# Five neighbouring weight rows to a partition in a fused layernorm, attention and gated-MLP kernel

## The chip, the cores and the metric

The kernel runs on one core of a Trainium2 chip. A core has a matrix engine (TensorE, PE in the profile; its weight loads are shown apart as PEld), a vector engine (VectorE, DVE), an activation engine (ScalarE, ACT), a general engine (GpSimd, POOL) and a queue processor that issues most transfers (SyncE, SP). The metric is the device time of one execution in microseconds. Before the change it is 308.31 us, the median of three runs (308.24 to 308.45).

## What is computed

The input x has 2048 rows (positions) of 640 features in bf16. The layernorm of x, called xn, feeds two branches, and the output is their sum with x:

```python
x = A_x
xn = _layernorm(x, axis=-1)
return x + _A_ref(xn, A_wqkv, A_wo) + _B_ref(xn, B_w_gate, B_w_up, B_w_down)
# A: qkv = xn @ wqkv (640 x 1920); 32 heads of 20; causal attention over a window
#    of 256 positions; the heads' outputs @ wo (640 x 640)
# B: (sigmoid(xn @ w_gate) * (xn @ w_up)) @ w_down, with 1536 hidden columns
```

The products with wqkv, w_gate and w_up sum over the 640 features. They are the ones that the change touches: such a sum can take the features in any order, as long as xn and the weight use the same one.

## The kernel before

**Tiling.** The 2048 positions are four chunks (c = 0 to 3) of 512, each of four blocks (s) of 128. The 640 features are cut into five tiles of 128 (DC = 5, index d), since a matmul sums over at most the 128 partitions. Tile d holds the features 128 d to 128 d + 127: feature f lies at partition f mod 128 of tile f div 128. All weights are loaded once and stay on chip as `[128 partitions, 5 tiles, columns]`. `wqkv_r` (line 163) is the view of the QKV weight that its loads take: `load_v` (line 181) reads the columns of V in two halves of 320, `load_wqkv` (line 171) those of Q and of K, 640 each, and `load_gu` (line 201) reads the gate and up weights, 384 columns at a time. In each of these loads a partition gets five pieces, one from each of five rows of the weight; a piece is 640, 1280 or 768 bytes long, which is only a part of its row (3840 bytes in wqkv, 3072 in gate and up).

**How xn gets its features onto partitions.** For chunk 0, at the start of the kernel, `transpose_rows` (line 296) has TensorE transpose each block: five transposes, each with 128 columns of the normed rows as the stationary operand (a PEld weight load) and an identity streaming through, then one copy out of PSUM into `xnT`. For the chunks 1 to 3, `g_norms` (line 385) takes the statistics of four blocks on VectorE and then norms them in `norm_block` (line 286), which writes the features of a row in the order "quarter q, tile b, 32 places f". `store_rows` puts these rows into a DRAM scratch, and `load_quarters` (line 305) reads them back, one quarter to 32 partitions. VectorE's 32 x 32 transposes in `turn_block` (line 313) then leave partition 32 q + f of tile b with the feature wanted. Between the last norm of a chunk and its `xnT` lie a store, a load and four turns.

**Order of the work.** The schedule is written by hand: the program order on every engine is the order in which the functions are called. At the start the queue SP issues the loads of x blocks 0, 1 and 3, the first half of V's weight, x block 2, the second half, Q and K, and then the first parts of gate and up. TensorE meanwhile runs some dummy matmuls (`keep_warm`), the transposes of block 0 and block 1, the first V product `v00` (line 695, ten steps of the loop at line 368 with block 1's), block 3's transposes, further V products, and so on; then the Q and K products of chunk 0 (`proj_block`, line 324). After that a generator machine (`Fill`) interleaves the attention steps with the pieces of everything else: gate/up of chunk 0, the norms and turns of chunk 1 beside them (lines 735 to 737), Q/K and V of chunk 1, the output of chunk 0, and so on. PSUM results lie in four buffers of `ps_d`, freed by copies on VectorE and ScalarE.

For chunk 0 the Q and K weights are read with a stride: `proj_block` views a slot of `wqk` as `"p (k m) -> p m k"`, so that consecutive columns of the stationary operand lie five elements (10 bytes) apart. For the later chunks GpSimd has sorted the columns (`sort_columns`) and they lie next to each other.

Of the kernel before, what the change touches and what calls it, by code (L numbers as in the profile page):

```python
# [9 lines left out]
P = 128  # L10
# [5 lines left out]
DC = D // P  # L16
# [10 lines left out]
FS = 768  # L27
# [85 lines left out]
def kernel(  # L113
# [11 lines left out]
    nc = tc.nc  # L125
# [34 lines left out]

    wqk = const.tile([P, 2 * DC + 1, D], BF16, name="wqk")
    wv = const.tile([P, DC, D], BF16, name="wv")
    wqkv_r = A_wqkv.rearrange("(c p) n -> p c n", p=P)
    wg = [const.tile([P, DC, FS], BF16, name=f"wg{k}") for k in range(F // FS)]
    wu = [const.tile([P, DC, FS], BF16, name=f"wu{k}") for k in range(F // FS)]
    wd = const.tile([P, FC, D], BF16, name="wd")
# [33 lines left out]

    def load_gu(t, w, k, lo=0, hi=FS):
        nc.sync.dma_start(out=t[k][:, :, lo:hi],
                          in_=w.rearrange("(c p) f -> p c f", p=P)[:, :, k * FS + lo:k * FS + hi])

    load_gu(wg, B_w_gate, 0, 0, FS // 2)
    load_gu(wu, B_w_up, 0, 0, FS // 2)
    clear("q")
    clear("k")
    load_gu(wg, B_w_gate, 0, FS // 2)

    def load_rest():
# [23 lines left out]
    ident = const.tile([P, P], BF16, name="ident")  # L235
# [27 lines left out]
    xns = {}  # L263
# [22 lines left out]
    def norm_block(c, s, mv, rstd):  # L286
        xn = lnp.tile([P, D], BF16, name="xn")
        made, of = xn, xc[c][:, s, :]
        if c:
            made = xn.rearrange("p (q b f) -> p b q f", q=4, b=DC)  # L290
            of = of.rearrange("p (b q f) -> p b q f", q=4, b=DC)
        nc.vector.tensor_scalar(out=made, in0=of, scalar1=mv[:, 0:1],
                                scalar2=rstd[:, 0:1], op0=SUB, op1=MULT)
        xns[c, s] = xn

    def transpose_rows(s, copy, lo=0, hi=DC):
        pt = ps_h.tile([P, DC, P], BF16, name="pt")
        for d in range(lo, hi):
            nc.tensor.transpose(pt[:, d, :], xns[0, s][:, d * P:(d + 1) * P], ident)  # L299
        copy(out=xnT[0][:, lo:hi, s * P:(s + 1) * P], in_=pt[:, lo:hi, :])  # L300

    def store_rows(c, s):
# [82 lines left out]
    def g_norms(c, behind=0):  # L385


        mvs = lnp.tile([P, SBC, nc.vector.BN_AGGR_DIM], FP32, name="mvs", bufs=1)
        for s in range(SBC):
            ln_block(c, s, mvs[:, s, :])  # L390
            if s < SBC - 1:
                yield 0
        for _ in range(behind):
            yield 0
        rstds = rstd_blocks(mvs)
        for _ in range(4):
            yield 0
        for s in range(SBC):
            norm_block(c, s, mvs[:, s, :], rstds[:, s:s + 1])
            store_rows(c, s)  # L400
            if s < SBC - 1:
                yield 0
# [126 lines left out]
    def scores(c, step):  # L529
        pt = pp.tile([P, HG, PTW], BF16, name="pT")  # L530
        ps = ps_s.tile([P, HG, CW], FP32, name="ps")
        for o, j, q, n, col in sorted(step["pieces"], key=lambda x: -x[3]):
            kc, kb = divmod(c * CW // U + j, CW // U)
            for a in range(2):
                for i in range(HG):
                    nc.tensor.matmul(  # L536
                        ps[a * U:(a + 1) * U, i, col * U:(col + n) * U],
                        lhsT=qk["k", kc, o // GH][32 * i:32 * i + DH, o % GH + a, kb * U:(kb + 1) * U],
                        rhs=qk["q", c, o // GH][32 * i:32 * i + DH, o % GH + a, q * U:(q + n) * U],
                        start=True, stop=True)  # L540
        nc.scalar.activation(out=pt[:, :, 0:CW], in_=ps, func=EXP, scale=SCALE)  # L541
        for diag, u, n in step["masks"]:
            base, sign = (0, 1) if diag else (-1, -1)
            for a in range(2):
                two = pt[a * U:(a + 1) * U].rearrange("p h (a b) -> p h a b", a=2)
                k, b = divmod(u, SPAN)
                view = two[:, :, k:k + n, b * U:(b + 1) * U]
                nc.gpsimd.affine_select(out=view, in_=view, pattern=[[0, HG], [0, n], [sign, U]],  # L548
                                        compare_op=GE, fill=0.0, base=base, channel_multiplier=-sign)
        if "late" not in step:  # L550
            return pt, None
        view = pt[:, :, step["late"] * U:(step["late"] + 2) * U]
        return pt, lambda: nc.vector.tensor_tensor(out=view, in0=view, in1=edge, op=MIN)
# [103 lines left out]
    def norm(s, mv, r):  # L657
        nc.vector.reciprocal(r, r)
        norm_block(0, s, mv, r)
# [29 lines left out]
    for lo, hi in ((0, 3), (3, DC)):  # L689
        transpose_rows(0, act, lo, hi)  # L690
    keep_warm(7)
    norm_act(1, xn1, neg1, r1)
    mv3 = ln_mv(ln_half(0, 3, 1, stats3))
    transpose_rows(1, dve)
    v00 = project_v(0, 0, 0)
    r3 = root(mv3)
# [3 lines left out]
    v10 = project_v(0, 1, 0)  # L700
    copy_v(0, 0, 0, v00, dve, (0,))
    transpose_rows(3, dve)
    v01 = project_v(0, 0, 1)
    norm_act(2, xn2, neg2, r2)
# [59 lines left out]
    for t, (c, k, step) in enumerate(todo):  # L764
# [11 lines left out]
        pt, late = scores(c, step)  # L776
# [13 lines left out]
    c = NCH - 1  # L790
# [62 lines left out]
```

## Time and profile before

| | us |
|---|---|
| median of three runs | 308.31 (308.24 to 308.45) |
| the profiled execution: its time | 308.43 |
| the profiled execution: its span on the core | 306.7 |
| VectorE busy in the span | 179.9 (59%) |
| ScalarE busy | 197.5 (64%) |
| GpSimd busy | 173.0 (56%) |
| DMA, all queues: bytes moved, mean rate | 36.04 MB, 118 GB/s |

The profile is of one execution. A busy time is the time in which an engine runs instructions. The chain of waits is found by going back from the last instruction, at each step to what released it. A row of the groups gives a line of the kernel, the engine, the operation, the tiles (written <- read), the shapes and the count; then the busy time in us and the mean of one in ns; then the idle time of the engine just before them and what ended it. A row of a timeline begins with the start and the length, in us from the span's start.

### The profile page before, as it was taken

How to read it: one execution, taken by the hardware profiler on the slowest of the kernel's cores; microseconds unless marked ns; L12 is line 12 of the kernel's file. 1: busy time of each engine (PE TensorE's matmuls, PEld its weight loads, DVE VectorE, ACT ScalarE, POOL GpSimd, SP SyncE). 2: the span in 40 equal slices, each digit the busy share in tenths (PEclk: the TensorE clock that was granted, in tenths of full speed). 3: DMA queues.
4: the chain of work that ended last, by engine and by line, in shares of the span. 5: the costliest groups of instructions: out<-in, count | busy, mean ns of one | idle time of the engine just before them, and what ended most of it. 6: DMA issues, size and time to landing. Idle time of an engine off the chain costs nothing.

```text
span 306.7 us, 10106 instructions
## 1 busy us (share of the span) xinstructions
PE 299.9 (98%) x4341; PEld 168.0 (55%) x4376; DVE 179.9 (59%) x356; ACT 197.5 (64%) x194; POOL 173.0 (56%) x314
## 2 busy tenths in 40 slices
PE   8999999999999999999999999999999999999996
PEld 6654444445657654554557654554546664444774
DVE  5735657889866569683826555482733527362433
ACT  6833768688965648888655538979585557778000
POOL 3086667479873728676572827657372756557000
DMA  7998959646574152773001222650000210000202
GB/s 209 364 316 253 320 185 260 206 129 194 141 231 111 44 161 83 235 221 75 4 0 47 65 70 80 193 177 2 2 2 2 66 45 25 0 4 0 88 24 64
DMA packets 40148, 36.04 MB, mean 118 GB/s; under 512 B 9000, under 2 KB 39848, under 8 KB 40104
## 3 DMA queue, kind: packets, MB, share of 16 engines
q1 hardware_dynamic: 39240, 34.63, 37.1%
q10 hardware_dynamic: 864, 0.77, 0.8%
q8 instruction: 34, 0.56, 0.8%
q14 instruction: 10, 0.08, 0.1%
HBM read 24.77 MB, written 10.62 MB: 115 GB/s over the span
## 4 chain that ended last, share of the span: by engine, by line
PE 96%; DMA 2%; issue 1%; SPq 0%; DVE 0%
PE y L481 18%; PE pu L467 17%; PE pg L460 17%; PE pqk L331 14%; PE ps L536 9%; PE pv L368 8%; PE y L488 7%; PE acc L567 6%; DMA wv<-in_A_wqkv_dram 2%; SPq L177 0%; PE pt L299 0%; DVE xn L492 0%
## 5 line engine op out<-in xcount | busy, mean ns | idle before, releaser
L548 POOL TENSOR_SCALAR_AFFINE_SELECT pT<-pT 64x512 bf16<-64x512 bf16 (+1 forms) x252 | 152.4, 605 | 90.7 <-ACT pT L541 79.0
L541 ACT ACTIVATE pT<-ps 128x2048 bf16<-128x2048 f32 x75 | 140.8, 1877 | 58.8 <-PE ps L536 57.8
L471 DVE SCALAR_TENSOR_TENSOR h<-th,pu 128x512 bf16<-128x512 f32 x48 | 32.7, 683 | 55.9 <-PE pu L467 42.7
L467 PE MATMUL pu<-xnT,wu 128*128 128x512 bf16 x230 | 58.9, 380 | 0.7 <-issue 0.3
L460 PE MATMUL pg<-xnT,wg 128*128 128x512 bf16 x225 | 58.3, 380 | 1.2 <-issue 0.6
L481 PE MATMUL y<-wd,h 128*128 128x320 bf16 (+2 forms) x396 | 56.6, 295 | 0.0
L331 PE MATMUL pqk<-xnT,wqk 128*128 128x512 bf16 x190 | 44.9, 380 | 0.7 <-issue 0.3
L481 PEld LDWEIGHTS <-h 128*128 128x128 bf16 x396 | 36.7, 98 | 15.9 <-issue 2.2
L463 ACT ACTIVATE th<-pg 128x512 f32<-128x512 f32 x48 | 28.6, 596 | 15.3 <-PE pg L460 15.1
L460 PEld LDWEIGHTS <-wg 128*128 128x128 bf16 x240 | 22.2, 98 | 25.7 <-issue 2.0
L467 PEld LDWEIGHTS <-wu 128*128 128x128 bf16 x240 | 22.1, 98 | 25.4 <-issue 1.8
L536 PE MATMUL ps<-qT,kT 20*64 20x320 bf16 (+4 forms) x1456 | 31.9, 259 | 0.0
L331 PEld LDWEIGHTS <-wqk 128*128 128x128 bf16 x200 | 19.5, 103 | 21.2 <-issue 1.2
L579 DVE STREAM_TRANSPOSE t<-acc 128x512 f32<-128x512 f32 x32 | 21.1, 695 | 13.7 <-PE acc L567 13.7
L536 PEld LDWEIGHTS <-kT 20*64 20x64 bf16 x1456 | 15.7, 103 | 24.5 <-issue 22.0
L492 DVE SCALAR_TENSOR_TENSOR rows<-y,rows 128x320 bf16<-128x320 f32 x30 | 14.3, 484 | 21.4 <-PE y L488 21.1
L368 PE MATMUL pv<-wv,xnT 128*128 128x320 bf16 x160 | 25.8, 300 | 0.3 <-DMA wv<-in_A_wqkv_dram 0.3
L488 PE MATMUL y<-wo,oc 128*128 128x320 bf16 (+2 forms) x165 | 24.2, 295 | 0.0
L567 PE MATMUL acc<-pT,v 64*32 64x320 bf16 (+4 forms) x1456 | 19.7, 252 | 0.0
L567 PEld LDWEIGHTS <-v 64*32 64x32 bf16 x1456 | 16.4, 91 | 5.9 <-ACT pT L541 1.3
L368 PEld LDWEIGHTS <-xnT 128*128 128x128 bf16 x160 | 14.6, 98 | 8.9 <-issue 1.6
L591 DVE TENSOR_TENSOR on<-t,rec 128x320 bf16<-128x320 f32 (+1 forms) x32 | 18.6, 580 | 1.1
(52 smaller groups left out, 187.8 us busy)
## 6 DMA issues: line engine op xcount, KB each, us to landing
qT<-sq SPq DMA_DIRECT2D x16, 256.0 KB
kT<-sk SPq DMA_DIRECT2D x16, 256.0 KB
sq<-st SPq DMA_DIRECT2D x20, 128.0 KB
sk<-st SPq DMA_DIRECT2D x20, 128.0 KB
out_dram<-rows SPq DMA_DIRECT2D x15, 160.0 KB
wg<-in_B_w_gate_dram SPq DMA_DIRECT2D x4, 480.0 KB
wu<-in_B_w_up_dram SPq DMA_DIRECT2D x4, 480.0 KB
xc<-in_A_x_dram SPq DMA_DIRECT2D x3, 640.0 KB
```

The lines of the kernel that those rows point to most:

```text
L331: nc.tensor.matmul(ps, lhsT=wt[:, m, :], rhs=xnT[c][:, d, :], start=(d == 0), stop=(d == DC - 1))
L368: nc.tensor.matmul(ps[:, 0:HALF], lhsT=xnT[c][:, d, s * P:(s + 1) * P], rhs=wv[:, d, hf * HALF:(hf + 1) * HALF], start=(d == 0), stop=(d = ...
L460: nc.tensor.matmul(pg, lhsT=part(wg, d, f), rhs=xnT[c][:, d, :], start=(d == 0), stop=(d == DC - 1))
L463: nc.scalar.activation(out=th, in_=pg, func=TANH, scale=0.5)
L467: nc.tensor.matmul(pu, lhsT=part(wu, d, f), rhs=xnT[c][:, d, :], start=(d == 0), stop=(d == DC - 1))
L471: nc.vector.scalar_tensor_tensor(out=h, in0=th, scalar=1.0, in1=pu, op0=ADD, op1=MULT)
L481: nc.tensor.matmul(y[:, 0:cut[1] - cut[0]], lhsT=ht[c, f][:, s * P:(s + 1) * P], rhs=wd[:, f, cut[0]:cut[1]], start=(f == 0), stop=False)
L488: nc.tensor.matmul(y[:, 0:cut[1] - cut[0]], lhsT=oc[c, m][:, s * P:(s + 1) * P], rhs=wo[:, m, cut[0]:cut[1]], start=False, stop=(m == DC - 1))
L536: nc.tensor.matmul(ps[a * U:(a + 1) * U, i, col * U:(col + n) * U], lhsT=qk["k", kc, o // GH][32 * i:32 * i + DH, o % GH + a, kb * U:(kb + ...
L541: nc.scalar.activation(out=pt[:, :, 0:CW], in_=ps, func=EXP, scale=SCALE)
L548: nc.gpsimd.affine_select(out=view, in_=view, pattern=[[0, HG], [0, n], [sign, U]], compare_op=GE, fill=0.0, base=base, channel_multiplier ...
L567: nc.tensor.matmul(acc[32 * i:32 * i + 32, q * U:(q + n) * U], lhsT=vt[kb][a * U:(a + 1) * U, u, h * VW:h * VW + 32], rhs=pt[a * U:(a + 1) ...
```

## The change

The rows of wqkv, w_gate and w_up go to partitions five neighbours at a time: partition p now gets the rows 5 p to 5 p + 4, in the tiles 0 to 4, where it had the rows p, 128 + p, 256 + p, 384 + p and 512 + p. Feature f thus lies at partition f div 5 of tile f mod 5. The columns that each load takes, the order of the loads and the number and size of the pieces are as before.

xn follows. In `norm_block`, for the chunks 1 to 3, the row of x is read in the order "quarter, 32 places, tile" and written where it was written before, so that consecutive elements written are five elements apart in what is read. In `transpose_rows`, for chunk 0, the 128 columns of a transpose are taken five elements apart. `turn_block`, `load_quarters`, all matmuls and the weights wd and wo are as they were.

```diff
-    wqkv_r = A_wqkv.rearrange("(c p) n -> p c n", p=P)
+    wqkv_r = A_wqkv.rearrange("(p c) n -> p c n", p=P)
...
         nc.sync.dma_start(out=t[k][:, :, lo:hi],
-                          in_=w.rearrange("(c p) f -> p c f", p=P)[:, :, k * FS + lo:k * FS + hi])
+                          in_=w.rearrange("(p c) f -> p c f", p=P)[:, :, k * FS + lo:k * FS + hi])
...
         made, of = xn, xc[c][:, s, :]
         if c:
             made = xn.rearrange("p (q b f) -> p b q f", q=4, b=DC)
-            of = of.rearrange("p (b q f) -> p b q f", q=4, b=DC)
+            of = of.rearrange("p (q f b) -> p b q f", q=4, b=DC)
         nc.vector.tensor_scalar(out=made, in0=of, scalar1=mv[:, 0:1],
                                 scalar2=rstd[:, 0:1], op0=SUB, op1=MULT)
...
         pt = ps_h.tile([P, DC, P], BF16, name="pt")
+        by_row = xns[0, s].rearrange("p (k d) -> p d k", d=DC)
         for d in range(lo, hi):
-            nc.tensor.transpose(pt[:, d, :], xns[0, s][:, d * P:(d + 1) * P], ident)
+            nc.tensor.transpose(pt[:, d, :], by_row[:, d, :], ident)
         copy(out=xnT[0][:, lo:hi, s * P:(s + 1) * P], in_=pt[:, lo:hi, :])
```

## The prediction

> **What bounds the kernel now.** I read the page's busy times and its chain first, then the waits, then the timeline of the first 14 us, where the changed loads and transposes run, and last the groups of the norms and turns.
>
> ```profile
> PE 299.9 (98%) x4341; PEld 168.0 (55%) x4376; DVE 179.9 (59%) x356; ACT 197.5 (64%) x194; POOL 173.0 (56%) x314
> ...
> PE 96%; DMA 2%; issue 1%; SPq 0%; DVE 0%
> ```
>
> TensorE runs for 299.9 of 306.7 us, and the chain that ended last is 96% TensorE. The change takes no matmul away. It can gain only from the 6.8 us in which TensorE stands, and the one DMA in the chain is one that it touches: the first half of V's weight.
>
> ```profile
> 5.30 0.45 PE L299 MATMUL pt<-ident,xn 128*128 128x128 bf16 x5
> 5.59 0.57 PE L247 MATMUL pwarm<-const-bfloat16-1.0 128*128 128x128 bf16 x7
> 6.44 0.45 PE L299 MATMUL pt<-ident,xn 128*128 128x128 bf16 x5 [0.28 <-DVE xn L675]
> 7.15 1.52 PE L368 MATMUL pv<-wv,xnT 128*128 128x320 bf16 x10 [0.25 <-DMA wv<-in_A_wqkv_dram]
> 8.50 0.44 PE L299 MATMUL pt<-ident,xn 128*128 128x128 bf16 x5
> 8.78 2.28 PE L368 MATMUL pv<-wv,xnT 128*128 128x320 bf16 x15
> 10.90 0.44 PE L299 MATMUL pt<-ident,xn 128*128 128x128 bf16 x5
> 11.18 2.31 PE L368 MATMUL pv<-wv,xnT 128*128 128x320 bf16 x15
> ```
>
> This is TensorE's timeline of the start. At 7.15 it has stood 0.25 us for that weight; from there on the groups follow one another without a gap. A later landing costs its whole delay, an earlier one gains at most 0.25 us: block 1's transposes stand ahead of it and end at 6.89.
>
> **The loads.** Each load has as many pieces, of the same size, as before (640 to a load; 640, 1280 or 768 bytes each): a piece is a part of a row, so neighbouring rows do not join. What changes is where the next piece lies: 3840 bytes on in wqkv (3072 in gate and up) where it was 128 rows on (491,520 bytes; 393,216). The trace's packet records bound what that can do. In V's load (1280 packets of 640 bytes) the 5th and the 95th percentile are both 32 ns. The median 1280-byte packet takes 55 ns in the Q and K loads, whose pieces lie 128 rows apart, and 55 ns in the loads of x, whose partitions read neighbouring rows. Two quite different row orders, one duration: a packet goes at the pace of its engine, not of its place in memory. The windows agree: the core's sixteen DMA engines are full after 7 us.
>
> ```profile
> 7.15:9.00 1.85, 1.85 (x17) 1.43 (x17) 1.34 (x5) 1.61 (x4) 0.00 (x0) 1.00 1.03 376
> 9.00:11.00 2.00, 2.00 (x17) 1.31 (x16) 1.69 (x5) 1.91 (x6) 0.00 (x0) 1.00 1.06 377
> ```
>
> The last three columns are the granted clock (1.00), the DMA share and GB/s. I take **0** for all loads. The bounds for V's first half: down, the 0.25 us wait. Up: packets of this size do at times take longer (the first 107 of them averaged 72 ns), so at 72 instead of 32 ns for 40 packets on each of 16 engines, 40 x 40 ns = 1.6 us.
>
> The other loads have cover: Q's weight, queued behind 1.44 MB of x and V, is all read by about 10 us and first needed at 13.2; K's at about 18.9, gate's at 23.9. At 376 GB/s the 0.82 MB of K take 2.2 us, so that they would have to go at a third of their rate before anything waits.
>
> **The 20 transposes of chunk 0.** Their weight loads become strided by five elements. The kernel already has such loads: Q and K of chunk 0 against later chunks.
>
> ```profile
> L331 PEld LDWEIGHTS <-wqk 128*128 128x128 bf16 x50 | 5.9, 117 | 4.8
> ...
> L331 PEld LDWEIGHTS <-wqk 128*128 128x128 bf16 x50 | 4.5, 98 | 5.6 <-DVE xnT L314 0.4 <-issue 0.4
> ```
>
> The first line is from the window 13 to 24.2 us (strided), the second from 54 to 75 us (dense): 117 against 98 ns, 19 ns more. Twenty times 19 ns is 0.38 us; a group of five, 0.10 us. Block 0's group is hidden: its `xnT` is copied at 6.43 and waits for V's weight to 7.15. Block 1's falls into the 0.26 us between 6.89 and 7.15. Those of blocks 3 and 2, at 8.5 and 10.9, stand in a full stream, and a transpose there is short, so that its weight load doesn't hide behind a long matmul: 2 x 0.10 = **+0.2 us**. The bounds are 0 (behind the matmul ahead, as in Q and K, whose 50 strided loads lie under matmuls at full pace) and 0.38 (all on the path, if V's weight lands early). The Trainium skill, SBUF — State Buffer, section on the DMA port swizzle (its note on cachelines), says that bf16 may be strided by up to eight elements for free; the sum by it would be 0.2 us less. The two rows above, 117 against 98, do not agree with it for a weight load.
>
> **The 12 norms of chunks 1 to 3.**
>
> ```profile
> L292 DVE TENSOR_SCALAR xn<-xc,mvs,rstds 128x640 bf16<-128x640 bf16 x12 | 6.9, 594 | 0.0
> L292 DVE TENSOR_SCALAR xn<-xc,mv,rstd 128x640 bf16<-128x640 bf16 x2 | 0.9, 446 | 0.1
> L314 DVE STREAM_TRANSPOSE xnT<-xc 128x640 bf16<-128x640 bf16 x12 | 9.6, 822 | 0.5 <-DMA xc<-xr 0.5
> L345 POOL COPY wqk<-wqk 128x640 bf16<-128x640 bf16 x10 | 9.1, 909 | 0.6
> ```
>
> The same 640 elements cost 446 ns dense on both sides (chunk 0), 594 ns written in 20 runs of 32. No row shows VectorE reading bf16 five apart. From below: 594 (no reason for a gain, the write stays). From above: 909, GpSimd's copy of 640 elements that reads with exactly this stride, on another engine. I take 750, about half-way and below VectorE's own 822 for a whole shuffle of the row: +156 ns each, 12 x 0.156 = 1.9 us of VectorE (bound 12 x 0.315 = 3.8), on an engine that idles 41% of the span. What hides it: TensorE runs ahead over four PSUM buffers while VectorE catches up.
>
> Where VectorE's lateness can show is chunk 1: its last norm (39.33) is followed by its store, the wait of SP for the stores (issue of the reload at 44.84), the reload and the turns.
>
> ```profile
> 51.10 1.57 DVE L314 STREAM_TRANSPOSE xnT<-xc 128x640 bf16<-128x640 bf16 x2 [0.50 <-DMA xc<-xr]
> ...
> 54.77 0.76 PEld L331 LDWEIGHTS <-wqk 128*128 128x128 bf16 x5 [0.43 <-DVE xnT L314]
> ```
>
> VectorE stood 0.50 us for the reload and TensorE's weight load 0.43 us for the last turn, so this chain has no slack left. The three norms before are absorbed (VectorE idles 0.90 us ahead of the gate product at 38.72); the fourth passes on its 0.16, at most 0.32 us. Queued behind the reload on SP are five loads of wd (47.26), needed at 82.4: covered. The stores themselves, though, queue behind other transfers (window 37 to 45 us: 233 GB/s), which can swallow the delay. I charge **+0.1 us**, bounds 0 and 0.32. Chunks 2 and 3 have no wait of TensorE on a turn: 0.
>
> **Sum.** 0 + 0.2 + 0.1 = +0.3 us on the profiled execution, 308.43 us (span 306.7 and 1.7 around it), gives 308.7; that execution lies 0.12 us above the median, so against the median 308.31 + 0.3 = **308.6 us**. A measurement of this kernel tells about 0.2%, 0.6 us, from no change; the forecast is within it.
>
> **Rivals.**
>
> *V's weight lands late* (slower). Place: the wait at 7.15. With the pieces of a partition side by side, the sixteen engines' first reads could crowd the same part of memory, and packets stay at 72 ns, not only the first. For it: the slow first packets. Against: 32 ns at both percentiles and the two equal 55 ns. Price up to 1.6 us, 310.2; half of it 309.4. It decides once the landing is over 0.3 us later, as the sum has 0.3 already.
>
> *VectorE too late* (slower). The norms cost 909 ns. Then chunk 1's chain takes 0.32 us, and at 126.25 and 127.67 two norms stand ahead of V copies which free PSUM, in a stretch where VectorE has worked from 114.8 to 123.3 without a gap: 2 x 0.315 = 0.63 us if the buffers give no cover. With 0.2 of transposes, +1.15: 309.5. Against: VectorE idles 2.36 us just before 125.65.
>
> *Transfers go better* (faster). V's half lands early (-0.25) and chunk 1's reload no longer ends a wait (-0.43), and strided weight loads hide: 308.31 - 0.68 = 307.6; with the transposes' 0.2, 307.8. Against: the equal packet times. This is what a rule of the Trainium skill would do, DMA: Bandwidth & Descriptors, section on latency and other measured facts: streams with a large power-of-two row pitch lose rate (207 GB/s at 512 KiB, 214 at full rate); the old pitch was 480 KiB, just off it, and 3% of V's 5 us would be 0.15 us. The 55 ns at pitches of 480 KiB and of one row do not bear it out.
>
> **How the numbers follow.** Forecast 0.50, all of it within 0.2%. V late 0.18 and VectorE late 0.18, both beyond it. Better transfers 0.14, of which 0.10 beyond -0.2% and 0.04 within. So faster 0.10, same 0.54, slower 0.36. The forecast's own range is 308.2 to 308.9. To leave out no more than two in ten it reaches down to 307.9, into the better transfers, and up to 309.9, past VectorE late and most of V late.
>
> **What would show it.** Right: weight loads at line 299 near 117 ns; `pv` starting at 7.0 to 7.3; line 292 near 750 ns with a TensorE busy time that stays at 300 us; the wait of line 331 on line 314 between 0.4 and 0.8 us. Wrong: a start of `pv` after 7.5; idle time of TensorE beyond 7.5 us; packets of 640 bytes off 32 ns; a norm above 909 ns.

## The result: slower by a third of a per cent, and less steady

| | before | changed |
|---|---|---|
| median of 17 runs, us | 308.25 (307.93 to 308.59) | 309.13 (308.56 to 310.17) |
| ratio, 95% interval | | 1.0033 (1.0023 to 1.0043) |
| the profiled execution: time / span, us | 308.43 / 306.7 | 308.93 / 307.1 |

The changed kernel takes 0.88 us more at the median. Its runs also spread over 1.6 us where those of before spread over 0.7. The profiled execution of the changed kernel lies 0.20 us below its median, that of before 0.18 above its own, so the two traces show 0.50 us of the loss only.

The changed kernel's busy times and its chain, from the page:

```profile
PE 300.0 (98%) x4341; PEld 168.0 (55%) x4376; DVE 181.4 (59%) x356; ACT 197.5 (64%) x194; POOL 175.0 (57%) x314
...
PE 94%; DMA 2%; DVE 1%; issue 1%; SPq 1%; DVEq 0%
```

TensorE's work is the same, VectorE has 1.5 us more, and so has GpSimd (2.0 us), which no line of the change touches. VectorE now has a share of the chain. Lines after 297 are one further down than before.

TensorE's timeline of the changed kernel at the start:

```profile
5.34 0.47 PE L300 MATMUL pt<-ident,xn 128*128 128x128 bf16 x5
...
6.79 1.60 PE L369 MATMUL pv<-wv,xnT 128*128 128x320 bf16 x10
8.23 0.44 PE L300 MATMUL pt<-ident,xn 128*128 128x128 bf16 x5
8.94 2.20 PE L369 MATMUL pv<-wv,xnT 128*128 128x320 bf16 x15 [0.26 <-DMA wv<-in_A_wqkv_dram]
```

The first V products start 0.36 us sooner than before: V's first half was there. That need not be the change: with the transposes alone changed, below, they start at 6.85, with the loads of before. But the wait has moved to V's second half, at 8.94. SP's issues say why that half can be later. First the kernel before, then the changed one:

```profile
2.19 0.43 SPq L181 DMA_DIRECT2D wv<-in_A_wqkv_dram  x1
2.67 0.52 SPq L177 DMA_DIRECT2D xc<-in_A_x_dram  x1
3.23 0.43 SPq L181 DMA_DIRECT2D wv<-in_A_wqkv_dram  x1
```
```profile
2.19 0.67 SPq L181 DMA_DIRECT2D wv<-in_A_wqkv_dram  x1
2.90 0.62 SPq L177 DMA_DIRECT2D xc<-in_A_x_dram  x1
3.57 0.56 SPq L181 DMA_DIRECT2D wv<-in_A_wqkv_dram  x1
```

An issue of V's load costs SP 0.67 and 0.56 us instead of 0.43, and the second half is issued 0.34 us later. The median packet of 640 bytes still takes 32 ns.

Then the norms of chunks 1 to 3 (minimum / median / maximum in ns):

```profile
L292 DVE TENSOR_SCALAR xn<-xc,mvs,rstds x12: 668/714/1146, 34.2 to 131.3; 128x640 bf16<-128x640 bf16 x12
```

The median is 120 ns above the 594 of before, the mean of the twelve is 792, and one norm took 1146. Comparing the starts of the 4341 matmuls of both traces one by one, the changed kernel is 0.16 us behind at 8.9 us and 0.05 at the first Q product. By 81 us it is 0.07 ahead, at 82 us it falls back by 0.12, and at 129 us by 0.33 for good. VectorE's timeline there, the kernel before and then the changed one:

```profile
126.25 0.60 DVE L292 TENSOR_SCALAR xn<-xc,mvs,rstds 128x640 bf16<-128x640 bf16 x1
126.77 0.98 DVE L377 CAST v<-pv 64x320 bf16<-64x320 f32 x2
127.67 0.59 DVE L292 TENSOR_SCALAR xn<-xc,mvs,rstds 128x640 bf16<-128x640 bf16 x1
128.19 0.41 DVE L553 TENSOR_TENSOR pT<-pT,edge 128x512 bf16<-128x512 bf16 x1
```
```profile
126.31 1.15 DVE L292 TENSOR_SCALAR xn<-xc,mvs,rstds 128x640 bf16<-128x640 bf16 x1
127.36 0.98 DVE L378 CAST v<-pv 64x320 bf16<-64x320 f32 x2
128.26 0.84 DVE L292 TENSOR_SCALAR xn<-xc,mvs,rstds 128x640 bf16<-128x640 bf16 x1
129.02 0.41 DVE L554 TENSOR_TENSOR pT<-pT,edge 128x512 bf16<-128x512 bf16 x1
```

The mask at line 554 ends at 129.43; before, it ended at 128.60. TensorE's weight loads for the attention product that reads the masked tile, before and then changed:

```profile
128.37 1.09 PEld L567 LDWEIGHTS <-v 64*32 64x32 bf16 x96 [0.26 <-DVE xn L292]
```
```profile
128.42 0.79 PEld L568 LDWEIGHTS <-v 64*32 64x32 bf16 x65 [0.26 <-DVE v L378]
129.48 0.37 PEld L568 LDWEIGHTS <-v 64*32 64x32 bf16 x31 [0.27 <-issue]
```

The 96 loads of the product, in one piece before, break off after 65 and go on at 129.48, 0.05 us after the mask's end. (The profile names no releaser there; that it was the mask is read from the times.) Beside the two long norms GpSimd was at work: two selects from 126.35 to 127.64, and two memsets at 128.23 that took 0.42 and 0.38 us instead of 0.24 and 0.20.

### The profile page after: what moved, and what is told of

Read it like the earlier page. It is cut to its first block, busy times and chain, and to the rows that moved or that the text cites. A ratio compares the mean times of both kernels' runs of the same rounds, so it can differ in the third digit from the quotient of the medians.

```text
span 307.1 us, 10106 instructions
## 1 busy us (share of the span) xinstructions
PE 300.0 (98%) x4341; PEld 168.0 (55%) x4376; DVE 181.4 (59%) x356; ACT 197.5 (64%) x194; POOL 175.0 (57%) x314
## 4 chain that ended last, share of the span: by engine, by line
PE 94%; DMA 2%; DVE 1%; issue 1%; SPq 1%; DVEq 0%
PE y L482 18%; PE pu L468 17%; PE pg L461 17%; PE pqk L332 14%; PE ps L537 9%; PE y L489 7%; PE pv L369 7%; PE acc L568 6%; DMA wv<-in_A_wqkv_dram 2%; SPq L177 1%; DVE xn L292 1%; DVE v L378 0%; DVE h L472 0%; SPq L181 0%; DVE pT L554 0%
## 5 line engine op out<-in xcount | busy, mean ns | idle before, releaser
L549 POOL TENSOR_SCALAR_AFFINE_SELECT pT<-pT 64x512 bf16<-64x512 bf16 (+1 forms) x252 | 154.1, 611 | 89.1 <-ACT pT L542 77.2
L489 PEld LDWEIGHTS <-oc 128*128 128x128 bf16 x165 | 15.6, 98 | 6.3 <-issue 0.4
```

The costliest lines, as they stand in the source:

```text
L489: nc.tensor.matmul(y[:, 0:cut[1] - cut[0]], lhsT=oc[c, m][:, s * P:(s + 1) * P], rhs=wo[:, m, cut[0]:cut[1]], start=False, stop=(m == DC - 1))
```

## The experiments

Theory A: the strided norms make the loss, by VectorE's lateness. Theory B: the loads make it. Theory C: the strided transposes do. The first four kernels take the change apart. Each ratio below, with its 95% interval, is to runs of the kernel before on the same chip (medians 308.18 to 308.22; of these 91 runs three are over 309).

**Norms alone.**

```diff
-            of = of.rearrange("p (b q f) -> p b q f", q=4, b=DC)
+            of = of.rearrange("p (q f b) -> p b q f", q=4, b=DC)
```

> The kernel before, with only the norms of chunks 1 to 3 reading five apart; loads and transposes of before, so that the features of these chunks meet the weight rows in another order and their sums are others. Theory A (the strided norms are the cost: one undisturbed is about 0.70 us instead of 0.59, one beside GpSimd's selects up to 1.15, and two of them stand ahead of the mask at line 553 near 128 us, whose lateness stops TensorE): the whole loss, +0.6 to +1.0 us against the kernel before, 308.9 to 309.3. Theory B (the loads: V's second half lands 0.3 us later, SP takes 0.67 instead of 0.43 us to issue V's first half): within 0.2 us of the kernel before. Theory C (the strided transposes): within 0.2 us of it.

Measured: 309.10 us (seven runs, 309.02 to 309.46), ratio 1.0029 (1.0018 to 1.0040). The whole median loss is here; as to the norms A holds. Its profiled execution, the longest of the seven, lost 1.04 us of span: 0.10 to 0.15 at the start, 0.33 again at 129 us, and 0.63 at 82 us, where the changed kernel's profiled execution lost 0.12. TensorE, then GpSimd, at that place, first the kernel before and then this one:

```profile
81.11 1.04 PE L567 MATMUL acc<-pT,v 64*32 64x320 bf16 x72
```
```profile
78.49 2.43 POOL L548 TENSOR_SCALAR_AFFINE_SELECT pT<-pT 64x512 bf16<-64x512 bf16 x4
```
```profile
81.22 1.15 PE L567 MATMUL acc<-pT,v 64*32 64x320 bf16 x68
82.57 0.32 PE L567 MATMUL acc<-pT,v 64*32 64x320 bf16 x4 [0.21 <-POOL pT L548]
```
```profile
79.03 3.49 POOL L548 TENSOR_SCALAR_AFFINE_SELECT pT<-pT 64x512 bf16<-64x512 bf16 x4
```

The product breaks off after 68 of its 72 and waits for a tile that GpSimd masks. Those four selects took 2.43 us before, 2.91 in the changed kernel's profiled execution and 3.49 here, beside chunk 2's norms (from 77.6 and from 80.5). The third of them alone took 0.45 us before, 0.81 in the changed kernel and 1.51 here, while the norms beside it kept 0.70 to 0.72. So the strided norms hold up GpSimd, too, which theory A did not have, and by how much differs between executions.

**Loads alone.**

```diff
-    wqkv_r = A_wqkv.rearrange("(c p) n -> p c n", p=P)
+    wqkv_r = A_wqkv.rearrange("(p c) n -> p c n", p=P)
...
-                          in_=w.rearrange("(c p) f -> p c f", p=P)[:, :, k * FS + lo:k * FS + hi])
+                          in_=w.rearrange("(p c) f -> p c f", p=P)[:, :, k * FS + lo:k * FS + hi])
```

> The kernel before, with only the loads of wqkv, gate and up taken five neighbours to a partition; norms and transposes of before, so that features and weight rows do not match and the sums are others. Theory A: within 0.2 us of the kernel before. Theory B: the whole loss, +0.6 to +1.0 us, with V's second half landing at 8.9 us instead of 8.6 and TensorE waiting for it. Theory C: within 0.2 us.

Measured: 308.27 us, ratio 1.0010 (0.9998 to 1.0022). The median moves by 0.06 us, against B. But three of the 11 runs came out at 309.08, 309.55 and 309.94.

**Transposes alone.**

```diff
-            nc.tensor.transpose(pt[:, d, :], xns[0, s][:, d * P:(d + 1) * P], ident)
+            nc.tensor.transpose(pt[:, d, :], xns[0, s].rearrange("p (k d) -> p d k", d=DC)[:, d, :], ident)
```

> The kernel before, with only the 20 transposes of chunk 0 taking every fifth column; loads and norms of before, so that chunk 0's features meet the weight rows in another order. Theory A: within 0.2 us of the kernel before. Theory C: +0.4 us or more. My prediction's own step: weight loads at 117 ns and +0.2 us. Theory B: within 0.2 us.

Measured: 308.17 us, ratio 1.0001 (0.9992 to 1.0009): no loss, against C, though the interval reaches up to 0.28 us. The weight loads did lengthen as expected:

```profile
L299 PEld LDWEIGHTS <-xn x20: 117/118/147, 5.4 to 10.9; 128*128 128x128 bf16 x20
```

**The change with dense norms.** The diff of the norms, undone.

> The changed kernel with only the norms of chunks 1 to 3 read as before, in runs of 32; loads and transposes stay changed, so the features of chunks 1 to 3 meet other weight rows. Theory A: the loss is gone, within 0.25 us of the kernel before, and the spread of its runs is that of before (about 0.6 us from lowest to highest) instead of 1.6. Theory B: +0.6 to +1.0 us remains. Theory C: the same remains.

Measured: 308.37 us, ratio 1.0011 (1.0000 to 1.0021). The median loss is gone, as A has it, but not the spread, against what A expected: 308.01 to 309.92, two of 12 runs over 309. So the change does two things: the norms move the median, and the loads of wqkv now and then add a microsecond (nine of the 35 runs that have them and dense norms are over 309: these 12, the 11 of the loads alone and 12 below). But not all of the spread is theirs: two kernels below that have the loads of before and strided norms spread as widely.

**The norms' partner.** The selects of the steps of chunks 1 to 3 are left out.

```diff
-        for diag, u, n in step["masks"]:
+        for diag, u, n in (() if c else step["masks"]):
```

> The changed kernel without GpSimd's masking selects (line 549) in the attention steps of chunks 1 to 3, so that these steps leave their masks out; chunk 0's steps, beside which chunk 1's norms run, keep them. Theory D (a norm that reads five apart shares a port of the memory with GpSimd: the two hold each other up, and the lateness of either reaches TensorE): chunk 1's four norms stay at 0.70 to 0.93 us, the eight of chunks 2 and 3 all come down to 0.66 to 0.72 us, none near 1.15, and the gap in TensorE's attention product near 129 us shrinks or goes. Rival E (a strided read alone takes a varying time): norms of up to 1.1 us remain in chunk 3.

Measured in one run, which tells nothing of the median: of chunk 3's norms, for which the selects were out, the first two fell from 1.15 and 0.84 us to 0.70, and the other two stayed at 0.72 and 0.67 (VectorE, then TensorE):

```profile
126.61 0.70 DVE L292 TENSOR_SCALAR xn<-xc,mvs,rstds 128x640 bf16<-128x640 bf16 x1
127.23 0.98 DVE L378 CAST v<-pv 64x320 bf16<-64x320 f32 x2
128.13 0.70 DVE L292 TENSOR_SCALAR xn<-xc,mvs,rstds 128x640 bf16<-128x640 bf16 x1
128.75 0.41 DVE L554 TENSOR_TENSOR pT<-pT,edge 128x512 bf16<-128x512 bf16 x1
```
```profile
128.73 1.29 PE L568 MATMUL acc<-pT,v 64*32 64x320 bf16 x96
```

The product of 96 runs in one piece, 1.29 us as before, and the stop is gone. Chunk 1's four norms, with their selects, stayed at 0.90, 0.70, 0.92 and 0.79. My expectation had misplaced chunk 2: its norms run beside steps of chunk 0, whose selects stayed, and the stop at 82 us was there (0.62 us; time 308.69). Theory D holds in that norm and selects hold each other up, and rival E falls; that a shared port does it is not shown.

**The same norms elsewhere.** The last number is where in the mix chunk 3's norms begin.

```diff
-    fill.add("v2", mix(mix(g_v(2), g_gu(1, 3, 7), 0, 1), norms[3], 1), 40 * 136 + 4 * GU)
+    fill.add("v2", mix(mix(g_v(2), g_gu(1, 3, 7), 0, 1), norms[3], 9), 40 * 136 + 4 * GU)
```

> The changed kernel with one number altered: the norms of chunk 3 begin eight pieces later, near 139 us instead of 126, where VectorE idles about 2 us at a time and no late mask is due; the same instructions, all results kept. Theory A/D (what costs is lateness of VectorE ahead of the mask near 129 us): the stop of 0.33 us there is gone, and the median falls by 0.2 to 0.4 us against the changed kernel, to 308.7 to 308.9. Rival (the norms cost by their added length wherever they stand): the time stays at 309.1.

Measured: 309.33 us (308.74 to 310.10, eight runs), ratio 1.0036 (1.0021 to 1.0050). The median did not fall: a miss, and with this spread no verdict. In its trace the stop at 129 us is gone, though one of the moved norms still took 1.16 us; the execution was 0.17 us behind at V's second half, lost 0.53 at chunk 1's turns, where VectorE waited 1.03 us for the reload, and 0.11 at 82 us. Up to 125 us this is the changed kernel's own program, so chunk 1's turns can cost that, too, in some executions. So the move was repeated where the loads are those of before:

> The kernel with only the strided norms (loads and transposes of before, chunks 1 to 3 get other sums), and in it the norms of chunk 3 eight pieces later. Its runs without the move lie close together (309.02 to 309.46), so the move can be told here. Theory A/D: the 0.33 us near 129 us goes, median 308.7 to 308.85. Rival (the norms cost by their added length wherever they stand): 309.1.

Measured: 308.81 us (12 runs, 308.21 to 309.94), against 309.10 without the move, ratio to before 1.0017 (1.0007 to 1.0027). The median fell by 0.3 us as expected, and ten of the 12 runs lie below the lowest without the move; but these runs spread over 1.7 us, and the two kernels ran on different chips. TensorE's product at that place is whole again:

```profile
128.92 1.29 PE L567 MATMUL acc<-pT,v 64*32 64x320 bf16 x96
```

One of the moved norms still took 1.16 us. So the cost of this stop lies in where a long norm stands, not in its length. The stop at 82 us stayed (0.62 us). Then chunk 2 alone:

```diff
-            of = of.rearrange("p (b q f) -> p b q f", q=4, b=DC)
+            of = of.rearrange("p (q f b) -> p b q f" if c == 2 else "p (b q f) -> p b q f", q=4, b=DC)
```

> The kernel before with only chunk 2's four norms reading five apart (chunk 2's features meet other weight rows). The profile with all twelve strided lost 0.5 us near 82 us, where the last of four selects on GpSimd ended late, and 0.33 us near 129 us. Theory D: the first part alone, +0.4 to +0.6 us, 308.6 to 308.8, with GpSimd's four selects before 82 us taking 2.9 to 3.5 us together instead of 2.4, and nothing near 129 us. Rival (the loss is made by all norms alike, 0.3 each chunk): 308.5.

Measured: 309.05 us (308.19 to 310.08), ratio 1.0024 (1.0014 to 1.0035), more than expected and unsteady. The trace shows the stop at 82 us, 0.63 us, with the stretched selects, and none at 129:

```profile
79.02 3.48 POOL L548 TENSOR_SCALAR_AFFINE_SELECT pT<-pT 64x512 bf16<-64x512 bf16 x4
```

The medians thus do not add up as the stops do: chunk 2 alone costs 0.83 us, and all twelve norms with the stop at 129 us removed cost 0.59. No run tells where chunk 2's other 0.2 us lie.

**Which loads make the high runs.** Each of the two lines of the loads' diff alone:

> The kernel before with only the loads of wqkv five neighbours to a partition (features and rows do not match, the sums are others). The loads changed together left the median alone, but 3 of 11 runs came out 0.8 to 1.7 us above the rest. Theory F (the crowding of first reads at the start, V's halves landing late): such runs appear here, in about one of four. Theory G (the gate and up loads): none here, spread about 0.6 us.

Measured: 308.40 us, four of 12 runs at 309.24 to 309.72, ratio 1.0015 (1.0002 to 1.0027). The profiled execution was one of the high ones, 309.32. TensorE's timeline of it:

```profile
6.86 1.60 PE L368 MATMUL pv<-wv,xnT 128*128 128x320 bf16 x10
8.30 0.44 PE L299 MATMUL pt<-ident,xn 128*128 128x128 bf16 x5
9.77 2.20 PE L368 MATMUL pv<-wv,xnT 128*128 128x320 bf16 x15 [1.03 <-DMA wv<-in_A_wqkv_dram]
```

TensorE stood 1.03 us for V's second half and started on it 0.99 us later than before; 0.85 us of that stayed to the end. The packets were not slow: V's 1280 took 35.9 ns at the mean, 36.5 in the kernel before. But the last 25 of them ended after 8.32 us, by which time all of the kernel before had ended, and the very last at 9.41.

> The kernel before with only the gate and up loads five neighbours to a partition (features and rows do not match, the sums are others). Theory F: no run more than 0.6 us above the lowest. Theory G: about one run of four 0.8 to 1.7 us above the rest.

Measured: 308.16 us (308.00 to 308.77), ratio 0.9998 (0.9990 to 1.0007): gate and up cost nothing that shows. The profiled execution is the highest (308.77): with dense norms and the wqkv loads of before, it lost 0.37 us at chunk 1's turns, where VectorE waited 0.89 us for the reload. So this place varies without the change as well.

> The kernel before with only the two loads of V's weight five neighbours to a partition (V's sums are others). Theory F (V's second half, landing late, makes the runs 0.8 to 1.7 us above the rest): about one run in four or three so, as with the whole of wqkv. Rival (the Q and K loads make them): none, spread about 0.6 us.

```diff
-        nc.sync.dma_start(out=wv[:, :, hf * HALF:(hf + 1) * HALF], in_=wqkv_r[:, :, a:a + HALF])
+        nc.sync.dma_start(out=wv[:, :, hf * HALF:(hf + 1) * HALF], in_=A_wqkv.rearrange("(p c) n -> p c n", p=P)[:, :, a:a + HALF])
```

Measured: 308.73 us (308.13 to 309.20), ratio 1.0012 (1.0003 to 1.0022). V's loads alone raise the time, but as seven of 12 runs 0.4 us and more above the lowest, none over 309.20, rather than a few far off, so that a share of the Q and K loads is not excluded; the execution profiled (308.85) waited 0.43 us for V's second half.

> The loads of wqkv five neighbours to a partition (sums are others), and in addition x block 3 loaded from ScalarE's queue, so that SP issues both halves of V's weight about 0.4 us sooner, which makes up for the 0.34 us by which the longer issues had put off the second half. Theory F1 (the late issue makes the late landing): no run over 308.9, spread of before. Theory F2 (the order of the reads makes it, not the issue): one run in four to three still 0.8 to 1.7 us above the rest.

```diff
-    load_rows(3, nc.sync)
+    load_rows(3, nc.scalar)
```

Measured: 308.63 us, 11 of 12 runs between 308.50 and 308.86, one at 309.24 against the expectation of none over 308.9; ratio 1.0011 (1.0003 to 1.0019). The high runs all but went. But the edit had a side effect. TensorE's timeline:

```profile
5.97 0.45 PE L299 MATMUL pt<-ident,xn 128*128 128x128 bf16 x5 [1.23 <-DVE xn L292]
...
7.40 1.60 PE L368 MATMUL pv<-wv,xnT 128*128 128x320 bf16 x10
...
9.12 2.28 PE L368 MATMUL pv<-wv,xnT 128*128 128x320 bf16 x15
```

Block 0's norm came 0.6 us later, so all V products did, and V's second half had 0.3 us more time for that reason as well. It is in line with the late issue as the cause (F1), and does not prove it against the order of the reads (F2). And the late issue can't be all of it. The loads alone, in their profiled execution (308.22), issued V's second half just as late as the high run of wqkv, 3.55 against 3.57, and TensorE had it in time. SP, then TensorE, of the loads alone:

```profile
3.55 0.56 SPq L181 DMA_DIRECT2D wv<-in_A_wqkv_dram  x1
```
```profile
8.53 2.25 PE L368 MATMUL pv<-wv,xnT 128*128 128x320 bf16 x15
```

In the seven traces with V's new order and the late issue, V's last piece ended at 8.17 to 9.41 us; in the six with the old order, at 7.64 to 8.44. An issue 0.34 us later is of the size of the shift between the middles of these ranges (8.57 and 8.32), but does not give 9.41. What holds up the last pieces in some executions stays open. No version beat the kernel before.

## Why the prediction was right and where it was wrong

The time lies in the range (307.9 to 309.9), 0.5 us above the forecast of 308.6. The likeliest case, no change beyond 0.2%, did not come: the kernel is slower by 0.33%, the side that had a chance of 0.36. It lies in the range because that reached past the rival of a late VectorE; the sum itself missed, with 0.2 us too much for the transposes and 0.8 too little for the norms partly cancelling.

- **What bounds the kernel:** right. TensorE's busy time stayed (300.0 us), and what was lost is idle time of it (7.1 us, 6.8 before).
- **The norms, +0.1 us:** this is the term that was mis-sized; alone they cost 0.9 us. The length was nearly right (750 forecast, 792 at the mean), but three of the twelve, at 919, 925 and 1146 ns, passed the 909 that I had named as a sign of being wrong. Wrong was "chunk 1", the place: in the profiled execution its wait of line 332 on line 315 is 0.4 us as before, and the reload is issued sooner (44.36 against 44.84), so that the longer norm did not reach it. Two other executions did lose time there, 0.53 us with strided norms and 0.37 with dense ones. And wrong was the cover, "TensorE runs ahead over four PSUM buffers": what TensorE waits for are not buffers but masked tiles, at 129 us behind two norms on VectorE and at 82 us behind four selects on GpSimd. I had counted a longer norm as VectorE's own affair.
- **Rival "VectorE too late":** the right place (126.25 and 127.67) and the right engine, priced 0.63 us there, measured 0.33; but TensorE waited for the mask, not for the V copies that it named; behind the norm at 127.67 the trace of before has the mask already, at 128.19. That GpSimd lengthens the norms, and is lengthened, it did not see.
- **The transposes, +0.2 us:** the size of a weight load was right (118 ns), the sum probably wrong: the median moved by 0.0 us, as the row of Q and K in the lower bound had it, though the runs alone don't exclude 0.2. In the traces the five transposes of block 3 and of block 2 still start 0.28 us ahead of the next V products with the strided loads, as before, so the longer loads hide there.
- **The loads, 0:** right for gate and up, and nearly so for the median (0.06 us with all loads changed, 0.2 with wqkv alone and 0.5 with V alone, where the intervals leave out zero). The packets' pace was right too. The rival "V's weight lands late" came in some runs, at the second half and not the first, with 1.03 us in the one that was caught, where I had up to 1.6. Its mechanism, slow packets, was not what the traces show; one step that I left out is the issue on SP, 0.24 us longer for the same number of pieces; why single pieces came later still is open.

## What to carry to other kernels

When an instruction on an engine with idle time gets longer, look for what is queued behind it and waited for: here 0.1 to 0.55 us more for each of twelve instructions cost 0.63 and 0.33 us of TensorE's time at two places in the profiled execution with the norms alone, nearly its whole loss, and moving four of the twelve took 0.3 us off the median. Count the engine that works beside it as well, since a longer or differently shaped read can lengthen both. And a load with the same bytes and pieces need not cost its queue the same issue time: where loads stand close ahead of their use, read the issues, not the packets alone.

## What the runs showed of the hardware

- A VectorE norm of 128 x 640 bf16 elements read densely takes 0.56 to 0.60 us, beside GpSimd's selects or not. Read five elements apart it takes 0.67 to 0.72 us without selects and up to 1.16 beside them, and four selects beside such norms take 2.55 to 3.49 us instead of 2.43. Which of the two is held up differs: in the run of the norms alone, chunk 2's norms kept 0.70 to 0.72 us and one select went from 0.45 to 1.51, while in chunk 3 a norm went to 1.13 and the four selects beside it took 2.55. The Trainium skill, SBUF — State Buffer, section on who interferes with whom, says that VectorE in a two-port mode and GpSimd share a pair of memory ports that one holds at a time. The strided norms and the selects agree with that, in that each is stretched beside the other. The dense norms, one source and one destination in the same memory, could by the conditions that it points to share the pair as well, and show no stretch; no run here tells why.
- SP took 0.43 us to issue a load of 640 pieces whose rows lay 128 apart, and 0.56 to 0.68 us for the same pieces from neighbouring rows, in every trace with that order; the load of x between them took 0.62 instead of 0.52.
